# Gated attention and two MLPs on one core: U narrowed in the first attention chunk, half of the shifts on ScalarE, pair 2 through PSUM

## The chip, the cores and the metric

The kernel runs on one core of one Trainium2 chip. The metric is the device time of one execution in microseconds (us); lower is better. The time given for a kernel is the median of its runs.

## The reference

The input is four batches of 768 positions. Three parts follow each other:

- A gated linear attention over 8 heads of 48. With `f = sigmoid(f_logit)`, the state is `state = f[t] * state + outer(k[t], v[t])`, and the output is `y[t] = q[t] @ state`. The heads side by side give `x` (768 x 384).
- A low-rank mix over positions and an MLP: `u = x + (x^T @ U @ V)^T` with rank 32, then `x = u + relu(u @ w_ch1) @ w_ch2` with a hidden width of 1536.
- A gated block: `h = gelu(x @ w_in)` is cut in two halves, one half is normalised and mixed over positions by `w_sg`, the halves are multiplied, `w_out` follows, and `x` is added.

The weights U, V, w_ch1, w_ch2, w_in and w_out arrive as float64. The kernel takes them apart itself, as 64-bit words, since the chip computes in 32 bits.

## The kernel before, in words

**Order.** The program runs the attention of batch 0 alone, in six chunks of 128 positions (loop over `c`, lines 569 to 594). Then for each batch b come two half-batches (`hf`) of the first MLP, each in twelve steps `f`; between the matmuls of these steps the attention of batch b+1 is filled in by `plan` (lines 628 to 652). The third part follows at the end. From line 554 on the order is written out by hand: each engine executes its instructions in the order in which the program lists them, and an instruction that waits holds up all that stand behind it on its engine.

**Narrowing.** A float64 tile lies in SBUF as pairs of 32-bit words, `low` and `high`. Four small operations make a float32 tile of it:

- `spread` (line 253): ScalarE rescales the high word into `z`.
- `shift` (line 246): the low word is shifted right by 29 bits. VectorE does it (line 251), or ScalarE does the same from the word's top byte (line 249; before the change for U and for the first half of V, `"u"` and `"v0"`).
- `merge` (line 257): two VectorE instructions (lines 260 and 261) join `z` and `low`, then the sign.

`use_first` is spread and shift with `z` in SBUF, `use_middle` the merge. `bank_first` and `bank_middle` (lines 301 and 306) do the same with `z` in two PSUM banks. `use_last` (line 278) splits the result into a rounded high part (ScalarE, line 290) and a rest (GpSimd, line 292); for U it is `load_u` (line 310), where ScalarE repeats U four times (line 313) and VectorE makes the rest of one copy (line 314). "Pair i" below is the two tiles of MLP step i, w_ch1's and w_ch2's; there are twelve, 0 to 11. They go through only once, ahead of and during batch 0's first half, and stay in SBUF.

**Where each is narrowed.** U in chunk 1, V's halves in chunks 2 and 3, pair 0 in chunk 4, pair 1 in chunks 4 and 5, pair 2 behind the last chunk (lines 601 and 602), pairs 3 to 11 by `narrow_ahead` (line 618) during steps 0 to 8 of the first half: in step f, pair f+3 is merged, pair f+2 gets its `use_last`, and pair f+4 its `bank_first`.

**Between attention and MLP.** `low_rank_sum(0, c)` (line 470) adds `U^T x` of a chunk on TensorE, in a bank kept open. The last one gives `hs` (lines 480 and 481). `add_ahead` and `hl_from` (lines 494 to 508) build `u` of the first half of batch 0 in the three `"at"` banks, split it into `uh` (ScalarE) and `ul` (VectorE), and copy it to `xT` (line 507). The copy is read again only at the end of the half.

**A step of the MLP** (`mlp`, line 512): nine matmuls into `ps_h` (line 81); ScalarE takes the relu `ah` (line 542), VectorE the rest `al` (line 543); then TensorE runs the nine matmuls of the previous step's second layer (line 523, into `ps_ch`), and then the step's fill follows. In steps 2 to 4 of batch 0's first half the fill has also one low-rank product for the second half (`low_rank_add`, lines 490 and 492).

**Banks.** PSUM has eight: two `"h"`, three `"ch"`, three `"at"`. A tile gets the bank that has been free longest; its first writer waits until the last reader of the tile before is done. The attention of batch 0 uses `"ch"` for its outputs and transposes and `"at"` for scans and scores.

Of the kernel before, what the change touches and what calls it, by code (L numbers as in the profile page):

```python
# [8 lines left out]
F32 = mybir.dt.float32  # L9
# [4 lines left out]
ACTF = mybir.ActivationFunctionType  # L14
ALU = mybir.AluOpType
# [12 lines left out]
KD = DM // 128  # L28
KF1 = FF1 // 128
KH = HF // 128  # L30
HT = S // 2
# [6 lines left out]
UNIT = 384  # L38
ALL = slice(None)
# [13 lines left out]
def kernel(  # L53
# [16 lines left out]
    vec, act, pool, pe = nc.vector, nc.scalar, nc.gpsimd, nc.tensor  # L70
# [62 lines left out]
    def fast(st):  # L133
# [5 lines left out]
        xT = [keepx.tile([128, KD, S], F32, name=f"xT{b}") for b in range(B)]  # L139

        def bank(kind, shape):
            n = {"h": 2, "ch": 3, "at": 3}[kind]
            return ps.tile(shape, F32, tag=kind, bufs=n, name="ps_" + kind)
# [27 lines left out]
        zs = at_cm.enter_context(sp("zs", 2, "right"))  # L171
# [16 lines left out]
        us = cst.tile([128, NCH, 128], F32R, name="us")  # L188
# [38 lines left out]
        raws = {}  # L227
# [16 lines left out]
                    raws[i].append((words[:, :, 0], words[:, :, 1], tops[:, :, 3]))  # L244

        def shift(i):
            for low, _, top in raws[i]:
                if i in ("u", "v0"):
                    act.activation(low, top, ACTF.Copy, scale=1.0 / 32, bias=-15.5 / 32)
                else:  # L250
                    vec.tensor_scalar(low, low, 29, None, op0=ALU.logical_shift_right)  # L251
# [2 lines left out]
            for z, (_, high, _) in zip(zs, raws[i]):  # L254
                act.activation(z, high.bitcast(F32), ACTF.Copy, scale=2.0 ** -112)

        def merge(i, dst, zs):
            for d, z, (low, high, _) in zip(dst, zs, raws[i]):
                di, zi = d.bitcast(I32), z.bitcast(I32)
                vec.scalar_tensor_tensor(zi, zi, 3, low, op0=ALU.logical_shift_left, op1=ALU.bitwise_or)  # L260
                vec.scalar_tensor_tensor(di, high, -2 ** 31, zi, op0=ALU.bitwise_and, op1=ALU.bitwise_or)  # L261

        ready = {}

        def z_tiles(i):
            z = zs.tile([128, 2, UNIT], F32, tag="z", name="z")
            n = NCH * R if i == "u" else UNIT
            return [z[:, x, :n] for x in range(len(raws[i]))]

        def use_first(i):  # L270
            ready[i] = z_tiles(i)
            spread(i, ready[i])
            shift(i)

        def use_middle(i):
            merge(i, ready[i], ready[i])

        def use_last(i):
            del raws[i]
            z = ready.pop(i)  # L280
            if i == "u":
                load_u(z[0])
            elif i in homes:
                load_v(int(i[1]) * UNIT, z[0])
            else:
                hl = [p.tile([128, 2, UNIT], F32R, tag=f"w{i}", name=n + str(i)) for p, n in ((w1p, "w1"), (wp, "w2"))]
                w1s[i] = [hl[0][:, x].rearrange("p (a b) -> p a b", a=KD) for x in range(2)]
                w2s[i] = [hl[1][:, x] for x in range(2)]
                for t, s in zip(hl, z):
                    act.activation(t[:, 0], s, ACTF.Copy)  # L290
                for t, s in zip(hl, z):
                    pool.tensor_tensor(t[:, 1], s, t[:, 0].bitcast(F32), op=ALU.subtract)  # L292
# [5 lines left out]

        banked = {}

        def bank_first(i):
            banked[i] = [bank("at", [128, UNIT]) for _ in range(2)]
            spread(i, banked[i])
            shift(i)

        def bank_middle(i):
            ready[i] = z_tiles(i)
            merge(i, ready[i], banked.pop(i))

        def load_u(z):  # L310
            z3 = z.rearrange("p (c r) -> p c r", c=NCH)
            u4 = us.rearrange("p c (i r) -> p c i r", i=4)
            act.activation(u4, z3[:, :, None, :].to_broadcast([128, NCH, 4, R]), ACTF.Copy)
            vec.tensor_tensor(u4[:, :, 2, :], z3, u4[:, :, 2, :].bitcast(F32), op=ALU.subtract)

        def load_v(i, z):
            c = slice(i, i + UNIT)
# [71 lines left out]
        def a_out(b, c):  # L389
            e = tiles[b, c]  # L390
            vv = e["v"]
            y = bank(kind(b), [128, DM])
            half = [slice(i, i + C // 2) for i in range(0, C, C // 2)]
            for h in range(H):
                for t in half:
                    pe.matmul(y[t, h * D:(h + 1) * D], lhsT=e["am"][h % 2][:, h // 2, t],  # L396
                              rhs=vv[:, h * D:(h + 1) * D], start=(h == 0), stop=(c == 0 and h == H - 1))
            if c:
                for p in range(NP):
                    for t in half:  # L400
                        pe.matmul(y[t, p * 2 * D:(p + 1) * 2 * D], lhsT=e["q"][:, p, t], rhs=T[:, p, :],  # L401
                                  start=False, stop=(p == NP - 1))
            x = aw.tile([128, DM], F32, tag="x", name="x", bufs=3)
            act.activation(x, y, ACTF.Copy)
            if b:
                xh[b, c] = aw.tile([128, DM], F32R, tag="xh", name="xh", bufs=3)
                xl[b, c] = aw.tile([128, DM], F32R, tag="xl", name="xl", bufs=3)
                split(xh[b, c], xl[b, c], x)
            else:
                xh[b, c] = x  # L410
            if c < NCH - 1:
                kv = bank(kind(b), [PR, NP, D] if b else [PR, NP, 2 * D])
                if not b:
                    for rows in (slice(0, 64), slice(64, PR)):
                        pe.matmul(kv[rows], lhsT=ident[:PR, rows], rhs=T, start=True, stop=False)
                for p in range(NP):
                    for j in range(2):
                        rows = slice(64 * j, 64 * j + D)
                        pe.matmul(kv[rows, p, :] if b else kv[rows, p, j * D:(j + 1) * D], lhsT=e["kt"][:, p, rows],  # L419
                                  rhs=vv[:, (2 * p + j) * D:(2 * p + j + 1) * D], start=bool(b),  # L420
                                  stop=bool(b) or p == NP - 1)
                e["kv"] = kv
            e["x"] = x
# [70 lines left out]
        def add_ahead(d):  # L494
            t = bank("at", [128, HT])
            pe.matmul(t, lhsT=ident, rhs=xT[0][:, d, 0:HT], start=True, stop=False)
            return t

        def hl_from(us):
            hi = work.tile([128, KD, HT], F32R, tag="uh", name="uh")  # L500
            lo = work.tile([128, KD, HT], F32R, tag="ul", name="ul")
            for d, t in enumerate(us):
                pe.matmul(t, lhsT=hs[0][:, d * 128:(d + 1) * 128], rhs=vs[:, 0:HT], start=False, stop=True)
            for d, t in enumerate(us):
                split(hi[:, d], lo[:, d], t, vec)
            for d, t in enumerate(us):
                act.activation(xT[0][:, d, 0:HT], t, ACTF.Copy)
            hl[0, 0] = (hi, lo)

        pend = [lambda: None]  # L510
# [54 lines left out]
        a_scores(0, 0)  # L565
        warm(2)
        a_decay(0, 2)
        inside = {1: "u", 2: "v0", 3: "v1", 4: 0}
        for c in range(NCH):
            if c + 2 < NCH:  # L570
                a_grow(0, c + 2)
            if c + 1 < NCH:
                a_scores(0, c + 1)
            if c:
                a_xt(0, c - 1)
            if c > 1:
                low_rank_sum(0, c - 2)
            if c in inside:
                use_first(inside[c])
                use_middle(inside[c])  # L580
            elif c == NCH - 1:
                low_rank_sum(0, c - 1)
                use_middle(1)
            a_out(0, c)
            if c + 3 < NCH:
                a_decay(0, c + 3)
            if c + 1 < NCH:
                a_state(0, c)
            if c == NCH - 1:
                use_last(0)  # L590
            elif c == NCH - 2:
                use_first(1)
            elif c in inside:
                use_last(inside[c])
        sums_up = [add_ahead(d) for d in range(1)]
        low_rank_sum(0, NCH - 1)
        use_last(1)
        sums_up += [add_ahead(d) for d in range(1, KD)]
        hl_from(sums_up)
        a_xt(0, NCH - 1)  # L600
        use_first(2)
        use_middle(2)
        load(1, 0)
        load(1, 1)
        get(*range(3, KF1))
        bank_first(3)

        def rest(b, c):
            a_xt(b, c)
# [6 lines left out]
                load(nb, nc3)  # L616

        def narrow_ahead(f):
            if 2 <= f < 2 + KD:
                low_rank_add(0, 1, f - 2, "at")  # L620
            if f + 3 < KF1:
                bank_middle(f + 3)
            if f + 2 < KF1:
                use_last(f + 2)
            if f + 4 < KF1:
                bank_first(f + 4)
# [370 lines left out]
```

## Time and profile before

| | us |
|---|---|
| median of 3 runs | 697.84 |
| lowest, highest | 697.01, 699.84 |
| the profiled execution | 696.48 |
| its span, first to last instruction | 694.7 |

| engine | busy us | share of the span |
|---|---|---|
| TensorE (PE) | 678.2 | 98% |
| VectorE (DVE) | 424.2 | 61% |
| ScalarE (ACT) | 266.6 | 38% |
| GpSimd (POOL) | 244.9 | 35% |

Times in rows are counted from the start of the span. In the rows L470 is line 470 of the kernel, `out<-in` the tiles written and read, `x9` the number of instructions put together in one row. A bracket at the end of a row tells how long the engine was idle before it and which instruction ended that. PEld is TensorE's weight load, SPq the queue of DMA issues.

### The profile page before, as it was taken

The page shows a single profiled execution, that of the slowest core. Times are in us where ns is not written, and L with a number is a line of the kernel's source. Part 1 is how long each engine was busy: PE and PEld are TensorE (multiplying, and loading weights), DVE is VectorE, ACT ScalarE, POOL GpSimd, SP SyncE. Part 2 cuts the span into 40 slices and gives each one's busy share as a digit, 9 for nine tenths or more (in the row PEclk, how much of TensorE's full clock was granted, in tenths as well). Part 3 has the DMA queues.
Part 4 walks back from the last instruction along what each step waited for, and adds up shares of the span by engine and source line. Part 5 has one row for each costly group of instructions (what it writes and reads, how often), then busy time and mean ns, then how long its engine had stood idle before and what let it go on. Part 6 is the DMA issues. An engine that isn't in the chain of part 4 may idle for free.

```text
span 694.7 us, 12756 instructions
## 1 busy us (share of the span) xinstructions
PE 678.2 (98%) x5155; PEld 641.5 (92%) x5155; DVE 424.2 (61%) x745; ACT 266.6 (38%) x551; POOL 244.9 (35%) x302
## 2 busy tenths in 40 slices
PE   8898999999999999999999999999999999999996
PEld 5667989999999999999999999899899999989996
DVE  7989996645546535546538841585675386358532
ACT  4685623331333232333234533563434255243410
POOL 5535742221321120421122542675344353435030
PEclk9999999999999999999999999999999999999999
DMA  9990013130122110130005421000010001001002
GB/s 327 395 385 8 1 59 115 58 115 0 59 75 97 59 58 1 58 108 9 1 4 162 121 69 58 23 1 1 0 69 1 1 0 69 1 1 68 1 1 73
DMA packets 21810, 47.10 MB, mean 68 GB/s; under 512 B 2544, under 2 KB 10352, under 8 KB 21744
## 3 DMA queue, kind: packets, MB, share of 16 engines
q1 hardware_dynamic: 21744, 46.21, 19.4%
q8 instruction: 42, 0.69, 0.4%
q14 instruction: 24, 0.20, 0.1%
HBM read 41.49 MB, written 4.72 MB: 67 GB/s over the span
## 4 chain that ended last, share of the span: by engine, by line
PE 86%; DMA 7%; DVE 5%; issue 0%; POOL 0%; ACT 0%; SPq 0%; DVEq 0%; ACTq 0%
PE ps_h L81 29%; PE ps_ch L523 19%; PE ps_ch L81 13%; PE ps_at L81 13%; DMA raw<-in_w_dram 4%; PE ps_at L369 3%; PE ps_at L396 3%; DVE z L261 2%; PE ps_at L401 1%; DVE ps_at L260 1%; PE ps_at L383 1%; DVE raw L251 1%; DMA xT<-in_fqk_dram 1%; PE ps_at L470 1%; PE ps_at L446 1%; PE ps_at L419 1%
## 5 line engine op out<-in xcount | busy, mean ns | idle before, releaser
L543 DVE SCALAR_TENSOR_TENSOR al<-ps_h,ah 128x384 fp32r<-128x384 f32 x96 | 53.3, 556 | 117.0 <-ACT ah L542 116.5
L81 PE MATMUL ps_h<-uh,w 128*128 128x384 f32 x576 | 120.5, 343 | 0.7 <-POOL w L292 0.7
L523 PE MATMUL ps_ch<-ah,w 128*128 128x384 f32 x576 | 115.5, 334 | 1.0 <-ACT ah L542 1.0
L523 PEld LDWEIGHTS ps_ch<-ah,w 128*128 128x128 f32 x576 | 101.1, 188 | 1.5 <-ACT ah L542 1.5
L81 PEld LDWEIGHTS ps_h<-uh,w 128*128 128x128 f32 x576 | 98.9, 188 | 2.8 <-POOL w L292 1.0
L542 ACT ACTIVATE ah<-ps_h 128x384 fp32r<-128x384 f32 x96 | 47.1, 490 | 121.7 <-PE ps_h L81 121.7
L523 PE MATMUL ps_ch<-al,w 128*128 128x384 f32 x288 | 65.8, 336 | 1.0 <-DVE al L543 1.0
L81 PE MATMUL ps_h<-ul,w 128*128 128x384 f32 x288 | 65.4, 334 | 0.0
L147 POOL TENSOR_TENSOR ul<-xT,uh 128x384 fp32r<-128x384 f32 x45 | 46.8, 1067 | 47.7 <-ACT uh L146 46.8
L147 POOL TENSOR_TENSOR gtl<-t,gth 128x384 fp32r<-128x384 f32 x32 | 32.7, 1024 | 73.6 <-ACT gth L146 73.6
L523 PEld LDWEIGHTS ps_ch<-al,w 128*128 128x128 f32 x288 | 51.2, 188 | 1.4 <-DVE al L543 1.3
L81 PEld LDWEIGHTS ps_h<-ul,w 128*128 128x128 f32 x288 | 51.5, 188 | 0.1
L342 POOL TENSOR_TENSOR fall<-g,fqk 112x4 f32<-112x4 f32 x18 | 3.7, 207 | 134.7 <-DVE g L338 134.7
L146 ACT ACTIVATE gth<-t 128x384 fp32r<-128x384 f32 x32 | 16.8, 525 | 78.0 <-DVE t L775 78.0
L375 DVE TENSOR_TENSOR am<-ps_at,mask 128x512 f32<-128x512 f32 x42 | 27.3, 685 | 19.5 <-PE ps_at L369 19.4
L147 POOL TENSOR_TENSOR vnl<-t,vnh 128x512 fp32r<-128x512 f32 x24 | 31.0, 1292 | 17.8 <-ACT vnh L146 17.8
L81 PE MATMUL ps_ch<-w,vnh 128*128 128x384 f32 x144 | 36.6, 335 | 0.0
L81 PE MATMUL ps_at<-w,vnh 128*128 128x384 f32 x144 | 36.6, 334 | 0.0
L147 POOL TENSOR_TENSOR xl<-x,xh 128x384 fp32r<-128x384 f32 x18 | 18.2, 1010 | 51.8 <-ACT xh L146 50.5
L292 POOL TENSOR_TENSOR w<-z,w 128x384 fp32r<-128x384 f32 x24 | 24.4, 1036 | 18.9 <-ACT w L290 15.0
L345 POOL TENSOR_TENSOR fqk<-fqk,g 112x512 f32<-112x512 f32 x21 | 27.0, 1285 | 6.7 <-DVE g L338 6.7
L369 PEld LDWEIGHTS ps_at<-fqk 48*128 48x128 f32 x336 | 21.7, 187 | 7.5 <-issue 4.4
(225 smaller groups left out, 1502.3 us busy)
## 6 DMA issues: line engine op xcount, KB each, us to landing
fqk<-in_fqk_dram SPq DMA_DIRECT2D x38, 384.0 KB, 3.8
raw<-in_w_dram SPq DMA_DIRECT2D x24, 384.0 KB, 7.8
out_dram<-xT SPq DMA_DIRECT2D x24, 192.0 KB, 1.9
v<-in_v_dram SPq DMA_DIRECT2D x21, 192.0 KB, 4.1
raw<-in_w_in_dram SPq DMA_DIRECT2D x8, 384.0 KB, 3.2
xT<-in_fqk_dram SPq DMA_DIRECT2D x6, 384.0 KB, 6.5
z<-in_w_sg_dram SPq DMA_DIRECT2D x12, 192.0 KB, 2.4
fqk<-in_fqk_dram SPq DMA_DIRECT2D x6, 256.0 KB, 4.7
```

The source lines that it names most:

```text
L81: pe.matmul(ps, lhsT=l, rhs=r, start=(i == 0), stop=(i == n - 1))
L146: act.activation(hi, src, ACTF.Copy)
L147: eng.tensor_tensor(lo, src, hi.bitcast(F32), op=ALU.subtract)
L261: vec.scalar_tensor_tensor(di, high, -2 ** 31, zi, op0=ALU.bitwise_and, op1=ALU.bitwise_or)
L292: pool.tensor_tensor(t[:, 1], s, t[:, 0].bitcast(F32), op=ALU.subtract)
L345: pool.tensor_tensor(k, k, g.rearrange("p h t -> p (h t)"), op=ALU.mult)
L369: pe.matmul(sc[j][:, p, :], lhsT=e["k"][rows, p, :], rhs=e["q"][rows, p, :], start=True, stop=True)
L375: vec.tensor_tensor(am, sc[j], m3, op=ALU.mult)
L396: pe.matmul(y[t, h * D:(h + 1) * D], lhsT=e["am"][h % 2][:, h // 2, t], rhs=vv[:, h * D:(h + 1) * D], start=(h == 0), stop=(c == 0 and h = ...
L523: pe.matmul(ch[d], lhsT=w, rhs=a[i // 2], start=(f == 0 and i == 0), stop=(last and i == 2))
L542: act.activation(ah, hp, ACTF.Relu)
L543: vec.scalar_tensor_tensor(al, hp, 0.0, ah.bitcast(F32), op0=ALU.max, op1=ALU.subtract)
```

## The change

1. `load_u`: the subtraction for U goes from VectorE to GpSimd.
2. U is narrowed one chunk sooner: spread and shift ahead of chunk 0's work, merge and `load_u` in chunk 0 instead of chunk 1.
3. `shift`: ScalarE takes also V's second half, and of each pair from 3 on the first tile (w_ch1's). VectorE keeps the second tile, and both tiles of pairs 0, 1 and 2.
4. Pair 2: spread (into one `"h"` and one `"ch"` bank) and shift in the last attention chunk; the two merges around `hl_from`; its `use_last` first in the fill of step 0.
5. The three copies to `xT` go from `hl_from` to the fill of step 0, behind the first relu; `bank_first(3)` follows them there, since the three `"at"` banks are taken until then.

```diff
         def shift(i):
-            for low, _, top in raws[i]:
-                if i in ("u", "v0"):
+            for x, (low, _, top) in enumerate(raws[i]):
+                if i in ("u", "v0", "v1") or i > 2 and x == 0:
                     act.activation(low, top, ACTF.Copy, scale=1.0 / 32, bias=-15.5 / 32)
                 else:
                     vec.tensor_scalar(low, low, 29, None, op0=ALU.logical_shift_right)
...
-        def bank_first(i):
-            banked[i] = [bank("at", [128, UNIT]) for _ in range(2)]
+        def bank_first(i, kinds=("at", "at")):
+            banked[i] = [bank(k, [128, UNIT]) for k in kinds]
             spread(i, banked[i])
             shift(i)
...
-            vec.tensor_tensor(u4[:, :, 2, :], z3, u4[:, :, 2, :].bitcast(F32), op=ALU.subtract)
+            pool.tensor_tensor(u4[:, :, 2, :], z3, u4[:, :, 2, :].bitcast(F32), op=ALU.subtract)
...
                 split(hi[:, d], lo[:, d], t, vec)
-            for d, t in enumerate(us):
-                act.activation(xT[0][:, d, 0:HT], t, ACTF.Copy)
             hl[0, 0] = (hi, lo)
...
-        inside = {1: "u", 2: "v0", 3: "v1", 4: 0}
+        inside = {0: "u", 2: "v0", 3: "v1", 4: 0}
         for c in range(NCH):
+            if c == 0:
+                use_first("u")
             if c + 2 < NCH:
                 a_grow(0, c + 2)
...
             if c in inside:
-                use_first(inside[c])
+                if c:
+                    use_first(inside[c])
                 use_middle(inside[c])
             elif c == NCH - 1:
                 low_rank_sum(0, c - 1)
                 use_middle(1)
+                bank_first(2, ("h", "ch"))
             a_out(0, c)
...
         low_rank_sum(0, NCH - 1)
         use_last(1)
-        sums_up += [add_ahead(d) for d in range(1, KD)]
-        hl_from(sums_up)
+        bank_middle(2, slice(0, 1))
+        ups += [add_ahead(d) for d in range(1, KD)]
+        hl_from(ups)
+        bank_middle(2, slice(1, 2))
         a_xt(0, NCH - 1)
-        use_first(2)
-        use_middle(2)
         load(1, 0)
         load(1, 1)
         get(*range(3, KF1))
-        bank_first(3)
...
         def narrow_ahead(f):
+            if f == 0:
+                use_last(2)
+                for d, t in enumerate(ups):
+                    act.activation(xT[0][:, d, 0:HT], t, ACTF.Copy)
+                bank_first(3)
             if 2 <= f < 2 + KD:
                 low_rank_add(0, 1, f - 2, "at")
             if f + 3 < KF1:
                 bank_middle(f + 3)
-            if f + 2 < KF1:
+            if 0 < f < KF1 - 2:
                 use_last(f + 2)
```

## Rows read from the trace of the kernel before

**Rows 1.** Busy by stretch: stretch, its us, each engine's busy us, PEclk, DMA share, GB/s

```profile
22.90:25.30 2.40, 0.03 (x2) 0.02 (x1) 2.40 (x2) 2.11 (x5) 2.11 (x3) 1.00 1.04 397
25.30:46.50 21.20, 21.20 (x322) 15.54 (x322) 18.07 (x29) 14.00 (x37) 8.71 (x9) 1.00 1.03 395
92.00:424.00 332.00, 331.14 (x2930) 318.81 (x2929) 189.04 (x323) 107.50 (x220) 84.56 (x106) 1.00 0.21 65
```

**Rows 2.** Timeline of TensorE, 22 to 27 us: start us, us, instruction

```profile
22.42 0.49 PE L446 MATMUL ps_ch<-ident,x 128*128 128x128 f32 x3
25.28 0.91 PE L470 MATMUL ps_h<-x,us 128*128 128x384 f32 x2 [2.37 <-DVE us L314]
```

**Rows 3.** Timeline of VectorE and GpSimd, 22 to 26 us

```profile
22.87 2.36 DVE L314 TENSOR_TENSOR us<-z,us 128x192 fp32r<-128x192 f32 x1 [0.28 <-ACT us L313]
23.74 1.27 POOL L378 TENSOR_TENSOR am<-am,mask 128x512 f32<-128x512 f32 x1
```

**Rows 4.** Timeline of ScalarE, 47 to 56 us

```profile
47.06 1.41 ACT L507 ACTIVATE xT<-ps_at 128x384 f32<-128x384 f32 x3
...
50.51 0.49 ACT L542 ACTIVATE ah<-ps_h 128x384 fp32r<-128x384 f32 x1
...
54.97 0.48 ACT L542 ACTIVATE ah<-ps_h 128x384 fp32r<-128x384 f32 x1
```

**Rows 5.** Timeline of TensorE, 47 to 76 us

```profile
47.70 0.74 PE L81 MATMUL ps_h<-ul,w 128*128 128x384 f32 x3
...
51.05 1.33 PE L523 MATMUL ps_ch<-ah,w 128*128 128x384 f32 x6 [1.02 <-ACT ah L542]
...
58.81 0.44 PE L490 MATMUL ps_at<-vs,hs 128*128 128x384 f32 x1 [1.41 <-DVE z L261]
...
62.47 0.44 PE L490 MATMUL ps_at<-vs,hs 128*128 128x384 f32 x1
...
72.67 1.20 PE L81 MATMUL ps_h<-uh,w 128*128 128x384 f32 x6
...
75.79 1.20 PE L81 MATMUL ps_h<-uh,w 128*128 128x384 f32 x6
```

**Rows 6.** Timeline, 62 to 91 us: VectorE, and TensorE's wait

```profile
62.33 0.63 DVE L251 TENSOR_SCALAR raw<-raw 128x384 int32<-128x384 int32 x2
...
80.10 1.54 DVE L251 TENSOR_SCALAR raw<-raw 128x384 int32<-128x384 int32 x2
...
85.47 1.62 DVE L338 TENSOR_TENSOR_SCAN g<-fqk,gone 112x511 f32<-112x511 f32 x1 [0.71 <-ACT fqk L331]
...
90.52 1.16 PE L369 MATMUL ps_at<-fqk 48*128 48x128 f32 x16 [1.02 <-POOL gmin L346]
```

**Rows 7.** Groups by line and shape, 11 to 92 us: busy, mean ns | idle before, releasers

```profile
L292 POOL TENSOR_TENSOR w<-z,w 128x384 fp32r<-128x384 f32 x24 | 24.4, 1036 | 18.9 <-ACT w L290 15.0 <-DMA raw<-in_w_dram 3.8
L251 DVE TENSOR_SCALAR raw<-raw 128x384 int32<-128x384 int32 x25 | 12.2, 530 | 0.0
L261 DVE SCALAR_TENSOR_TENSOR z<-raw,ps_at 128x384 int32<-128x384 int32 x18 | 10.0, 555 | 1.2
L255 ACT ACTIVATE ps_at<-raw 128x384 f32<-128x384 f32 x18 | 9.2, 517 | 9.9 <-DVE z L261 7.5 <-DVE xT L492 2.4
```

**Rows 8.** DMA issues of U: the timeline's row, and KB and us to landing

```profile
7.21 0.33 SPq L241 DMA_DIRECT2D raw<-in_w_u_dram  x1
...
raw<-in_w_u_dram SPq DMA_DIRECT2D x1, 192.0 KB, 5.4
```

**Rows 9.** Timeline of ScalarE and VectorE in the attention, single instructions

```profile
13.29 0.60 ACT L377 ACTIVATE am<-ps_at 128x512 f32<-128x512 f32 x1 [1.27 <-PE ps_at L369]
24.42 0.59 ACT L249 ACTIVATE raw<-raw 128x384 int32<-128x384 uint8 x1
42.82 0.49 ACT L404 ACTIVATE x<-ps_ch 128x384 f32<-128x384 f32 x1 [1.15 <-PE ps_ch L401]
44.84 0.55 DVE L481 TENSOR_TENSOR hs<-ps_h,hs 32x384 fp32r<-32x384 f32 x1 [1.31 <-ACT hs L480]
```

More of the change, by code (lines that the diff above doesn't have):

```diff
@@ L255, in spread, with merge @@
                 act.activation(z, high.bitcast(F32), ACTF.Copy, scale=2.0 ** -112)
-        def merge(i, dst, zs):
-            for d, z, (low, high, _) in zip(dst, zs, raws[i]):
+        def merge(i, dst, zs, only=ALL):
+            for d, z, (low, high, _) in list(zip(dst, zs, raws[i]))[only]:
                 di, zi = d.bitcast(I32), z.bitcast(I32)
@@ L299, in fast, with bank_middle @@
         banked = {}
-        def bank_first(i):
-            banked[i] = [bank("at", [128, UNIT]) for _ in range(2)]
+        def bank_first(i, kinds=("at", "at")):
+            banked[i] = [bank(k, [128, UNIT]) for k in kinds]
             spread(i, banked[i])
             shift(i)
-        def bank_middle(i):
-            ready[i] = z_tiles(i)
-            merge(i, ready[i], banked.pop(i))
+        def bank_middle(i, only=ALL):
+            if i not in ready:
+                ready[i] = z_tiles(i)
+            merge(i, ready[i], banked[i], only)
         def load_u(z):
@@ L594, in fast @@
                 use_last(inside[c])
-        sums_up = [add_ahead(d) for d in range(1)]
+        ups = [add_ahead(0)]
         low_rank_sum(0, NCH - 1)
         use_last(1)
-        sums_up += [add_ahead(d) for d in range(1, KD)]
-        hl_from(sums_up)
+        bank_middle(2, slice(0, 1))
+        ups += [add_ahead(d) for d in range(1, KD)]
+        hl_from(ups)
+        bank_middle(2, slice(1, 2))
         a_xt(0, NCH - 1)
-        use_first(2)
-        use_middle(2)
         load(1, 0)
```

## The prediction, made before the changed kernel was run

> **What bounds the kernel now.** First the table of busy time by stretch [rows 1]. From 92 us to 424 us TensorE is busy in 331.14 of 332.00 us, and the change touches nothing there, so the question is the first 92 us. The stretch from 22.90 to 25.30 us stands out: TensorE does almost nothing in it. Right behind it, from 25.30 to 46.50 us, it is busy without a gap (21.20 of 21.20 us) while VectorE (18.07) and ScalarE (14.00) have room. So in the attention TensorE waits once and then sets the pace to the end.
>
> The timeline names that wait: the first low-rank sum, line 470, starts at 25.28 us after 2.37 us of idling for `us`, VectorE's subtraction on line 314 [rows 2]. That subtraction has 192 columns and takes 2.36 us, from 22.87 to 25.23 us; it ends just after GpSimd's mask product, which runs from 23.74 to 25.01 us [rows 3]. It does not compute for 2.36 us, it is held up by GpSimd's work.
>
> Next the entry of the MLP. Step 0's first layer is done at 48.44 us (47.70 + 0.74), but its relu `ah` starts only at 50.51 us: ScalarE first does three copies to `xT` (1.41 us), pair 2 and pair 3. The relu of step 1 starts at 54.97 us [rows 4, 5]. TensorE waits 1.02 us for the first relu, and at 58.81 us 1.41 us for a merge on VectorE, whose bank the low-rank product needs. Steps 2 and 3 with such a product take 3.66 us (62.47 - 58.81), plain steps 3.12 us (75.79 - 72.67), which is TensorE's own pace [rows 5].
>
> Last, at the end of the narrowing, a pair of shifts that takes 0.63 us undisturbed takes 1.54 us; a scan idles 0.71 us for a sigmoid, and TensorE waits 1.02 us ahead of the first scores of batch 1 [rows 6].
>
> The chain of waits is no help before 48 us: it runs through DMAs that had landed long before their readers started.
>
> **The change part by part.**
>
> *U sooner, and its subtraction on GpSimd.* With `us` ready, the sum on line 470 follows the transposes that end at 22.91 us (22.42 + 0.49), 2.37 us sooner [rows 2]. On GpSimd the subtraction costs some 0.52 us, half of the 1036 ns of 384 columns on line 292 [rows 7]; it stands ahead of a mask product that is read a whole chunk later. VectorE loses the 2.36 us and keeps U's two merges, a chunk earlier. Since TensorE was gapless from there on, the whole of it should arrive at the end of the attention: **-2.4 us**. Between the ends, 0 (another wait takes the place) and -2.4, I take the upper one because VectorE, which feeds TensorE, loses as much.
>
> The Trainium skill (GPSIMD Engine Reference, section 4.1 Engine selection) says otherwise for such an operation: elementwise work belongs on VectorE, GpSimd being about twice as slow with two inputs. By it this edit would lose some 0.26 us and the sum would be about -1.0 us. The row decides against it: 2.36 us on VectorE here.
>
> New waits by it: ScalarE's spread for U now waits for U's DMA with all of chunk 0 queued behind it. It is issued at 7.21 us and lands 5.4 us later, at 12.6 us [rows 8]. ScalarE idles 1.27 us before 13.29 us [rows 9], and the two short instructions fit almost exactly. Each us of later landing would push the attention by up to one, of which VectorE's 2.4 us of new room takes some. No DMA changes its place in SP's queue.
>
> *V's second half shifted by ScalarE.* 0.59 us more there [rows 9], a shift less on VectorE; TensorE is the bound in that chunk [rows 1], so 0. Were ScalarE late, 0.6 us at most.
>
> *Pair 2 in the last chunk.* Two spreads of 0.52 us come ahead of the copy at 42.82 us, before which ScalarE idles 1.15 us; two shifts on VectorE come ahead of the subtraction at 44.84 us, before which it idles 1.31 us [rows 9]. Cost 0; with the cover gone some 0.1 to 0.5 us. The first half of the merge has the gap behind that subtraction, the second the one ahead of `al` of step 0. Both banks are free: the last chunk holds two of three `"ch"` and one of two `"h"`.
>
> *The entry.* The relu of step 0 now starts when its matmuls are done, at 48.44 - 2.37 = 46.07 us, and the first wait of 1.02 us is gone. But its queue behind that relu has grown: `ah`, two copies of pair 2, three copies to `xT`, two spreads of pair 3 and two of pair 4, ten instructions at 0.46 us from start to start (the three copies: (1.41 - 0.49) / 2), and two shifts at 0.5 us. The second spread of pair 4 waits for a bank that the merge of pair 3's first tile frees, two instructions of 0.555 us [rows 7] behind ScalarE's own shift, less the 0.46 us of the first spread: 0.65 us idle. Together 4.6 + 1.0 + 0.65 = 6.25 us, so the relu of step 1 starts at 52.3 us, not 54.97: -2.65 us in all, and beyond the attention's share only **-0.3 us**. Then VectorE does `al` and four merges: 0.49 + 0.55 + 4 x 0.555 us, with small overlaps 3.25 us; the low-rank product starts at 55.6 us, not 58.81: another **-0.5 us**. Ends for both: +0.5 (a wait of ScalarE's usual 1.1 us, below) and -1.5 us (no such wait).
>
> *The steps.* VectorE's sum falls by one shift of 0.3 us, to 3.35 us with a product. But ScalarE's shift now closes a loop: second spread 0.52, shift 0.59, relu 0.48, `al` 0.55, product 0.55, the first tile's merge 1.11, and again; 3.8 us, less four overlaps of 0.1 and three handovers of 0.05 added, 3.55 us. In plain steps 3.1 us, beside TensorE's 3.12. So **-0.2 us** for two steps; ends -0.6 (VectorE's sum) and +0.6 (no overlap). Step 6 has three more copies on ScalarE for the next half and no room for them in this loop: **+0.2 us**, between 0 and 1.4 (three at 0.46).
>
> *The end of the narrowing.* One shift instead of two can be held up, so the last merges, the sigmoid and the scan come sooner relative to TensorE, which recovers part of its 1.02 us [rows 6]: **-0.5 us**, between 0 and -1.0.
>
> Beyond 92 us: 0, with 0.5 us either way for where GpSimd and VectorE happen to meet.
>
> **Sum:** -2.4 - 0.3 - 0.5 - 0.2 + 0.2 - 0.5 = **-3.7 us**, so 692.8 us for the profiled execution (696.48 us). The median of the runs is 1.36 us above that one, so the forecast for the median is 697.84 - 3.7 = **694.1 us**.
>
> **The rivals.**
>
> *The stall only moves.* With `us` early, something else holds the second chunk. For: VectorE is nearly full there, 2.40 of 2.40 us [rows 1]. Against: 2.36 of these are the stall itself. Half of the -2.4 lost gives 695.3, all of it 696.5.
>
> *The entry gives nothing.* ScalarE's queue in step 0 is longer than I count (6.25 us with a guess for the wait), and what the steps win goes to it. The attention's share alone remains: about 695.4.
>
> *ScalarE closes the loop on every step* (slower). Its spreads idled 9.9 us for VectorE [rows 7], over nine steps 1.1 us each, harmless so far. If that wait stays while a shift is added, a step is 0.48 + 4 x 0.517 + 0.59 us less five overlaps of 0.1, so 2.6, plus 1.1: 3.7 us against 3.12 in six plain steps, +3.5 us. With -2.4 - 0.8, +0.2 and no recovery at the end that is +0.5 us: 698.3. It decides where the second spread of a pair waits for a merge that starts behind ScalarE's own shift. For: that shift stands last in ScalarE's step. Against: the merge of pair f+3 needs a shift of the step before. The Trainium skill (ScalarE: Activation LUTs, section Rules for kernel authors) sides with this rival: simple arithmetic belongs on VectorE, not on ScalarE.
>
> *The change doesn't do what it says.* Pairs 0 to 2 keep both shifts on VectorE, so "one tile of each pair" holds for nine pairs of twelve; that is counted. 2%.
>
> **How the numbers follow.** Two runs of this kernel can be told apart at about 0.5%, 3.49 us here, so faster means below 694.35. The forecast lies 0.25 us under that. It has 0.55 (0.44 of it below 694.35), the moved stall 0.17, the idle entry 0.18, the ScalarE loop 0.08, the last 0.02. Faster 0.47 (0.03 from the others), same 0.48, slower 0.05 (the loop together with a late U). The range goes down to -4.8 us (entry -1.5, end -1.0 and part of the steps) and up to -0.6 us, where the moved stall and the idle entry meet in part: 693.0 to 697.2.
>
> **What would show it.** Right: line 470 starts near 22.9 us with no wait; TensorE gapless to the MLP; the first `ah` near 46.1 and the second near 52.3 us; the low-rank product at 55.6; steps with a product at 3.55 us; a wait under 0.6 us ahead of batch 1's scores, which start near 86.8. Wrong: a new gap of TensorE between 12 and 44 us; the second `ah` at 52.6 or later; plain steps over 3.2 us.

## The result, and the profile after

The changed kernel takes 691.60 us (median of 4 runs, 691.03 to 692.40); the kernel before took 698.38 us beside it (4 runs, 697.01 to 699.84). The ratio is 0.9903, interval 0.9879 to 0.9928: faster by 6.8 us. Forecast were 694.1 us and a range of 693.0 to 697.2 us, so the sign is right, the size too small, and the range missed it.

The two profiled executions lie closer together than the medians: 696.48 us before, 692.03 us after (spans 694.7 and 690.2 us), 4.5 us apart. The remaining 2.3 us is no part of a comparison of these two traces. Where it comes from is the main question of the experiments.

First the attention. Busy time by stretch, after:

```profile
22.90:25.30 2.40, 2.40 (x52) 1.78 (x52) 2.37 (x4) 1.56 (x5) 2.00 (x3) 1.00 1.04 399
25.30:46.50 21.20, 21.20 (x286) 15.86 (x282) 19.40 (x34) 16.91 (x44) 9.87 (x10) 1.00 1.03 395
```

and the timelines of TensorE at the first low-rank sum (line 471 now), of GpSimd at U's subtraction, of ScalarE at U's spread:

```profile
22.28 0.49 PE L447 MATMUL ps_ch<-ident,x 128*128 128x128 f32 x3
22.61 0.81 PE L471 MATMUL ps_h<-x,us 128*128 128x384 f32 x2
...
19.23 0.60 POOL L315 TENSOR_TENSOR us<-z,us 128x192 fp32r<-128x192 f32 x1
...
12.75 0.37 ACT L255 ACTIVATE z<-raw 128x192 f32<-128x192 f32 x1 [0.88 <-DMA raw<-in_w_u_dram]
```

The stretch in which TensorE did nothing [rows 1] is filled, and the sum follows the transposes without a wait. The subtraction takes 0.60 us on GpSimd, against 2.36 us on VectorE [rows 3]. ScalarE waits 0.88 us for U's DMA with chunk 0 behind it, as the prediction feared, but TensorE is busy for all of 12 to 22 us, so it costs nothing.

Next the entry and the steps. Timelines of ScalarE, VectorE and GpSimd from 41 to 53 us:

```profile
41.54 0.49 ACT L481 ACTIVATE hs<-ps_h 128x384 fp32r<-128x384 f32 x1 [0.18 <-PE ps_h L471]
...
45.80 0.49 ACT L541 ACTIVATE ah<-ps_h 128x384 fp32r<-128x384 f32 x1 [1.01 <-PE ps_h L81]
...
47.02 1.24 ACT L624 ACTIVATE xT<-ps_at 128x384 f32<-128x384 f32 x3
...
50.86 0.52 ACT L255 ACTIVATE ps_at<-raw 128x384 f32<-128x384 f32 x1 [0.89 <-DVE z L261]
51.31 0.54 ACT L249 ACTIVATE raw<-raw 128x384 int32<-128x384 uint8 x1
51.74 0.48 ACT L541 ACTIVATE ah<-ps_h 128x384 fp32r<-128x384 f32 x1
...
46.80 1.22 DVE L251 TENSOR_SCALAR raw<-raw 128x384 int32<-128x384 int32 x1
49.60 0.57 DVE L260 SCALAR_TENSOR_TENSOR ps_at<-ps_at,raw 128x384 int32<-128x384 int32 x1 [1.58 <-ACT raw L249]
...
46.78 2.11 POOL L292 TENSOR_TENSOR w<-z,w 128x384 fp32r<-128x384 f32 x2 [1.85 <-ACT w L290]
```

Of VectorE and ScalarE the groups by line, 11 to 92 us, that changed most:

```profile
L251 DVE TENSOR_SCALAR raw<-raw 128x384 int32<-128x384 int32 x15 | 7.9, 541 | 0.0
L255 ACT ACTIVATE ps_at<-raw 128x384 f32<-128x384 f32 x18 | 9.2, 519 | 5.6 <-DVE z L261 4.8 <-DVE xT L493 0.8
```

VectorE has ten shifts less [rows 7], and ScalarE's spreads idle 5.6 us instead of 9.9. TensorE, 46 to 87 us:

```profile
46.67 0.68 PE L81 MATMUL ps_h<-ul,w 128*128 128x384 f32 x3
...
52.27 1.31 PE L522 MATMUL ps_ch<-ah,w 128*128 128x384 f32 x6 [1.80 <-ACT ah L541]
...
55.06 0.44 PE L491 MATMUL ps_at<-vs,hs 128*128 128x384 f32 x1 [0.95 <-DVE z L261]
...
58.65 0.44 PE L491 MATMUL ps_at<-vs,hs 128*128 128x384 f32 x1
...
79.25 1.20 PE L81 MATMUL ps_h<-uh,w 128*128 128x384 f32 x6
...
82.37 1.20 PE L81 MATMUL ps_h<-uh,w 128*128 128x384 f32 x6
...
85.99 1.16 PE L370 MATMUL ps_at<-fqk 48*128 48x128 f32 x16 [0.34 <-issue]
```

The lead over before, event by event, begins with `hs`, for which the row of before is this:

```profile
44.32 0.49 ACT L480 ACTIVATE hs<-ps_h 128x384 fp32r<-128x384 f32 x1 [0.18 <-PE ps_h L470]
```

`hs` comes at 41.54 instead of 44.32 us (2.78 us), the second relu at 51.74 instead of 54.97 (3.23) [rows 4], the first low-rank product at 55.06 instead of 58.81 (3.75) [rows 5], the first scores of batch 1 at 85.99 instead of 90.52 (4.53) [rows 6]. From there to the end the lead stays what it is: the last instruction of VectorE starts at 684.40 instead of 688.95 us (4.55). From the end of that instruction to the end of the span the twelve profiles need 4.4 to 5.6 us, so two spans can differ by 1 us by that end alone; where it matters below, profiles are compared at that instruction instead. The wait for the first relu is gone; the one for the second is now the longest, 1.80 us, because ScalarE carries more between the two relus. Plain steps keep TensorE's pace (82.37 - 79.25 = 3.12 us).

### The profile page after: what moved, and what is told of

It reads as the page before. It is cut to its first block, busy times and chain, and to the rows that moved or that the text cites. A ratio compares the mean times of both kernels' runs of the same rounds, so it can differ in the third digit from the quotient of the medians.

```text
span 690.2 us, 12745 instructions
## 1 busy us (share of the span) xinstructions
PE 677.4 (98%) x5155; PEld 641.4 (93%) x5155; DVE 418.5 (61%) x734; ACT 270.9 (39%) x561; POOL 244.8 (35%) x303
## 4 chain that ended last, share of the span: by engine, by line
PE 93%; DVE 3%; ACT 2%; issue 1%; POOL 1%; DMA 0%; DVEq 0%; POOLq 0%; ACTq 0%
PE ps_h L81 30%; PE ps_ch L522 20%; PE ps_ch L81 14%; PE ps_at L81 14%; PE ps_at L370 4%; PE ps_at L397 3%; PE ps_at L402 1%; PE ps_at L384 1%; PE ps_at L471 1%; PE ps_ch L397 1%; PE ps_at L447 1%; PE ps_at L420 1%; ACT raw L249 1%; DVE z L261 1%; PE ps_h L471 1%
```

## The experiments

Three theories stood for the 2.3 us between medians and profiles:

- **Clock.** In most runs of the kernel before, TensorE falls to half clock behind its 2.4 us of idling for `us`; the profiled execution was one in which it didn't. The change takes that away too.
- **Held instructions.** The runs of before differ in how long VectorE's instructions are held up by GpSimd's.
- **Other parts.** The entry or the shifts bring more in most runs than in the profiled one.

The expectations of the first set of runs were written before the clock was suspected; it became a theory with that set's first profile. Times are medians; the kernel before had 698.03, 697.68 and 697.79 us beside the three sets of runs.

### The kernel before once more (first set)

No edit.

> The kernel before, unchanged, beside itself. It is to show what its runs differ by: its profiled execution took 696.48 us, its median 1.9 us more. Theory A (the parts gave what the profiles show, -4.5 us, and the rest of the difference between the medians is the spread of the kernel before): ratio 1.000 within 0.002, single runs 696.5 to 700, and a profile that differs from the earlier one inside the first 92 us by up to 2 us, in how long blocked VectorE instructions take. Theory B (the profiles miss something after 92 us that the change also moved): the first 92 us agree within 0.5 us and what differs lies later.

Measured: 698.41 us (12 runs, 696.74 to 699.87), ratio 1.0001 [0.9990, 1.0013]. The profiled execution was a typical one this time, 698.97 us with a span of 697.2 us. Its timeline shows the same wait, and its table by stretch (TensorE's busy time and granted clock, the last but two of the numbers) what follows it:

```profile
25.28 1.01 PE L470 MATMUL ps_h<-x,us 128*128 128x384 f32 x1 [2.38 <-DVE us L314]
```

```profile
22.90:25.30 2.40, 0.02 (x2) 0.85 1.04 397
25.30:26.30 1.00, 1.00 (x2) 0.50 1.05 393
26.30:30.30 4.00, 4.00 (x51) 0.50 1.03 394
30.30:31.30 1.00, 1.00 (x8) 0.50 1.04 393
31.30:32.30 1.00, 1.00 (x27) 0.95 1.04 397
```

The granted clock falls before the wait is over (0.85 in the first row) and is 0.50 for some 6 us behind it (1.2 GHz, the lower of the two levels), where the first profile of before had 1.00 in all of it [rows 1]. VectorE's subtraction lasts as long as ever (2.37 us from 22.86 us). The first relu,

```profile
53.35 0.49 ACT L542 ACTIVATE ah<-ps_h 128x384 fp32r<-128x384 f32 x1
```

comes 2.84 us later than the 50.51 us of the first profile [rows 4], about half of the 6 us, and the last instruction of VectorE 2.89 us later (691.84 against 688.95). So between these two executions the difference arises ahead of the MLP, by the clock and not by held instructions. The other runs have a mean granted clock each, and it goes with their time: of the 64 runs of this kernel in the three sets, the eleven with 0.999 or more took 695.31 to 696.74 us, the fifty with 0.997 or less 696.93 to 699.87 us.

The Trainium skill (TensorE: Matmul & The Clock Gate, Part 1, "What's actually happening") puts it so: "the default state is throttled, and activity releases the throttle." The rows above agree, with the two levels it names; that the same 2.4 us gap brings the fall in one execution and not in another is what the two profiles of before add.

### Only U sooner (first set)

The kernel before with parts 1 and 2 of the change alone:

```diff
-            vec.tensor_tensor(u4[:, :, 2, :], z3, u4[:, :, 2, :].bitcast(F32), op=ALU.subtract)
+            pool.tensor_tensor(u4[:, :, 2, :], z3, u4[:, :, 2, :].bitcast(F32), op=ALU.subtract)
...
-        inside = {1: "u", 2: "v0", 3: "v1", 4: 0}
+        inside = {0: "u", 2: "v0", 3: "v1", 4: 0}
         for c in range(NCH):
+            if c == 0:
+                use_first("u")
```

> The kernel before with parts 1 and 2 of the change alone (U in chunk 0, its subtraction on GpSimd). By the forecast -2.4 us, all of it at the low-rank sum of chunk 0, which then starts near 22.8 us, and no more later: ratio 0.9965. If the stall only moved: ratio over 0.998. If the U parts carry most of the measured 6.8 us: ratio 0.993 or less.

Measured: 693.19 us (5 runs, 692.74 to 693.82), ratio 0.9933 [0.9918, 0.9948]: 4.8 us, twice the length of the wait, and the runs spread over 1.1 us instead of 3. In its profile the clock is 1.00 from 12 to 92 us. The first low-rank product,

```profile
56.04 0.44 PE L490 MATMUL ps_at<-vs,hs 128*128 128x384 f32 x1 [1.41 <-DVE z L261]
```

comes 2.77 us sooner than in the profile of before [rows 5]. So 2.8 us of the 4.8 are the stall, and some 2.1 us aren't in a comparison with an execution that kept its clock.

### Without the shifts, and without the new entry (first set)

The changed kernel with the shifts of pairs 3 to 11 on VectorE again (V's second half stays on ScalarE):

```diff
-                if i in ("u", "v0", "v1") or i > 2 and x == 0:
+                if i in ("u", "v0", "v1"):
```

> The changed kernel with both shifts of pairs 3 to 11 back on VectorE (V's second half stays on ScalarE). If ScalarE's queue in step 0 is the bound there, as forecast, two shifts less bring the second relu 1.0 us sooner, from 51.7 to 50.7 us, and the steps are then 3.66 us instead of 3.59 where they have a product; at the end of the narrowing two shifts can be held up again, 0.5 to 0.9 us: the same time as the changed kernel within 1 us. If the shifts on ScalarE are what freed VectorE from GpSimd (the rival): 2 us or more slower than the changed kernel.

Measured: 691.93 us (691.41 to 692.40), ratio 0.9914 [0.9899, 0.9929]. And with parts 4 and 5 taken back, so that U and the shifts are left:

```diff
-                bank_first(2, ("h", "ch"))
...
-        bank_middle(2, slice(0, 1))
-        ups += [add_ahead(d) for d in range(1, KD)]
-        hl_from(ups)
-        bank_middle(2, slice(1, 2))
+        sums_up += [add_ahead(d) for d in range(1, KD)]
+        hl_from(sums_up)
         a_xt(0, NCH - 1)
+        use_first(2)
+        use_middle(2)
...
+        bank_first(3)
...
-            if f == 0:
-                use_last(2)
-                for d, t in enumerate(ups):
-                    act.activation(xT[0][:, d, 0:HT], t, ACTF.Copy)
-                bank_first(3)
```

> The changed kernel with parts 4 and 5 undone: pair 2 and the copies to xT as before, U and the shifts as changed. Forecast: the second relu is 0.3 to 1 us later than in the changed kernel (the relu of step 0 near 48.5 us, the one of step 1 near 52.5 us), and the kernel slower than the changed one by 0.8 us; if the blocked shift of pair 3 (1.44 us for two in the kernel before) stays, by 1.5 us. If the entry is worth nothing, the same time.

Measured: 691.29 us (690.76 to 691.73), ratio 0.9905 [0.9890, 0.9920], so not the 0.8 us above the changed kernel that were forecast: at least level with it. TensorE's waits at the entry, first without the shifts, then with the old entry:

```profile
51.15 1.32 PE L522 MATMUL ps_ch<-ah,w 128*128 128x384 f32 x6 [0.78 <-ACT ah L541]
54.46 0.44 PE L491 MATMUL ps_at<-vs,hs 128*128 128x384 f32 x1 [1.40 <-DVE z L261]
```

```profile
48.63 1.32 PE L523 MATMUL ps_ch<-ah,w 128*128 128x384 f32 x6 [1.46 <-ACT ah L542]
54.81 0.44 PE L490 MATMUL ps_at<-vs,hs 128*128 128x384 f32 x1 [0.93 <-DVE z L261]
```

On top of U alone the shifts bring 1.9 us (693.19 - 691.29) and the entry 1.3 us (693.19 - 691.93). Both together bring 1.6 us (the ratios 0.9933 and 0.9903 are 2.1 us apart, the two spans 691.8 and 690.2 us 1.6). They don't add: the first product comes at 54.46 us with the entry alone, 54.81 with the shifts alone and 55.06 with both. What the shifts bring on their own lies there (56.04 to 54.81) and in the 1.0 us ahead of batch 1's scores, which the kernel without shifts keeps and the one with the old entry doesn't.

### U's subtraction on VectorE, one chunk sooner (second set)

```diff
-            pool.tensor_tensor(u4[:, :, 2, :], z3, u4[:, :, 2, :].bitcast(F32), op=ALU.subtract)
+            vec.tensor_tensor(u4[:, :, 2, :], z3, u4[:, :, 2, :].bitcast(F32), op=ALU.subtract)
```

> The changed kernel with U's subtraction back on VectorE, still in chunk 0. It then queues behind VectorE's scan for chunk 3 and runs against GpSimd's products. If the engine is what mattered: the subtraction is held up by 1 to 2.5 us again and delays the scores of chunk 3, a wait of TensorE of 1 to 2 us near 21 us, and the kernel is 1 to 4 us slower than the changed one (the larger if the clock falls too). If the earlier place alone does it: the same time as the changed kernel.

Measured: 695.29 us (10 runs, 693.42 to 698.17), ratio 0.9966 [0.9947, 0.9986], 3.7 us of the gain gone (against 691.60 us; the two ratios are 4.4 us apart, `hs` in the two profiles 3.98 us, 45.52 against 41.54). Timelines of VectorE and TensorE, and the stretch behind:

```profile
17.91 2.73 DVE L315 TENSOR_TENSOR us<-z,us 128x192 fp32r<-128x192 f32 x1
...
22.61 1.71 PE L370 MATMUL ps_at<-xT 48*128 48x128 f32 x16 [1.87 <-issue]
...
25.00:30.00 5.00, 5.00 (x72) 0.66 1.04 395
```

The prediction's rival "the stall only moves" is what happens here. VectorE is held for 2.73 us, until 20.64 us, just behind GpSimd's three instructions, which run from 17.79 to 20.44 us; the scan, the products and the mask behind it come late, TensorE idles 1.87 us ahead of the next scores, and the clock falls behind that as well. The runs lie between 693.42 us, with a mean granted clock of 1.0, and 698.17 us with 0.99. So the earlier place alone doesn't remove the stall; what the engine does without it is the next question.

### U on GpSimd, but in chunk 1 as before (second set)

```diff
-        inside = {0: "u", 2: "v0", 3: "v1", 4: 0}
+        inside = {1: "u", 2: "v0", 3: "v1", 4: 0}
         for c in range(NCH):
-            if c == 0:
-                use_first("u")
```

> The changed kernel with U back in chunk 1, its subtraction on GpSimd. There it stands behind the key product of chunk 4 (to 23.6 us) and takes 0.5 us: the low-rank sum starts near 24.3 us, TensorE waits 1.4 us instead of 2.4 or none. 1.4 us slower than the changed kernel if the clock stays, up to 4 us if it falls behind a wait of that length as well. If the place doesn't matter: the same time as the changed kernel.

Measured: 693.29 us (5 runs, 692.69 to 693.50), ratio 0.9940 [0.9919, 0.9962].

```profile
24.27 0.91 PE L471 MATMUL ps_h<-x,us 128*128 128x384 f32 x2 [1.47 <-POOL us L315]
...
25.00:30.00 5.00, 5.00 (x93) 1.00 1.03 394
```

The subtraction stands behind a decay product on GpSimd and TensorE waits 1.47 us. The clock stays in this profile. `hs` comes 1.77 us later than with the whole change (43.31 against 41.54 us), the last instruction of VectorE 1.69 us (686.09 against 684.40), and the medians are as far apart (693.29 and 691.60 us): this shorter gap cost about its own length. So the engine alone leaves some 1.5 us of the wait, and it takes the engine and the earlier place together to remove it.

### The wait filled with products that nobody reads (second set)

The kernel before, with idle products in TensorE's queue ahead of the first low-rank sum. They are extra work; their results go nowhere.

```diff
+            if c == 2:
+                warm(3)
             if c > 1:
                 low_rank_sum(0, c - 2)
```

> The kernel before with three products of the identity with itself (some 2.2 us of TensorE work that nobody reads) ahead of the low-rank sum of chunk 0, where TensorE waits 2.4 us for U. The wait itself stays; only its idleness goes. Theory C (the idle wait costs twice: its 2.4 us, and in most runs a stretch behind it in which TensorE is granted half its clock, 0.50 from 25 to 31 us in the second profile of the kernel before, 2.5 us longer in all): the granted clock stays 1.00 from 22 to 46 us, the median falls to 696.6 us, ratio 0.998, and the runs lie within 1 us instead of 3. Rival (the clock has nothing to do with the spread of the runs): the same median and spread as the kernel before.

Measured: 696.12 us (12 runs, 695.34 to 696.49), ratio 0.9983 [0.9971, 0.9995].

```profile
22.42 2.10 PE L551 MATMUL ps_h<-ident 128*128 128x384 f32 x6
24.97 0.91 PE L470 MATMUL ps_h<-x,us 128*128 128x384 f32 x2 [0.44 <-DVE us L314]
...
26.30:30.30 4.00, 4.00 (x82) 1.00 1.04 397
```

This is the direct test of the clock. The low-rank sum still has to wait for `us`, starting 0.31 us sooner (by no work of the products: chunk 1's scores are 0.33 us sooner already, at 11.75 instead of 12.08 us), yet the median falls by 1.6 us and the spread from 4.3 us (24 runs of before beside it, 695.31 to 699.59) to 1.15 us. The lowest run is the same, 695.34 against 695.31; only the long ones are gone: 18 of the 24 runs of before lie above the highest of these twelve. The profiled execution is the lowest of the twelve, so its full clock proves little by itself; the spread of the twelve says more. Extra work makes this kernel faster.

### ScalarE's shifts only from pair 5 on (second set)

```diff
-                if i in ("u", "v0", "v1") or i > 2 and x == 0:
+                if i in ("u", "v0", "v1") or i > 4 and x == 0:
```

> The changed kernel with the shift of the first tile on ScalarE only from pair 5 on; pairs 3 and 4, whose shifts stand in step 0 between the first and the second relu, are shifted by VectorE. If ScalarE's queue in step 0 (5.9 us from relu to relu in the changed kernel) is the bound there: the second relu comes 1.0 us sooner, near 50.7 us, the wait of TensorE ahead of it shrinks from 1.8 to 0.8 us, and the kernel is 0.5 to 1.0 us faster than the changed one, near 690.8 us. If VectorE, which then has two shifts against GpSimd, is the next bound: the same time.

Measured: 691.41 us (6 runs, 690.50 to 691.46), ratio 0.9912 [0.9892, 0.9932]: no difference that can be told.

```profile
46.77 2.30 DVE L251 TENSOR_SCALAR raw<-raw 128x384 int32<-128x384 int32 x2
...
51.21 1.32 PE L522 MATMUL ps_ch<-ah,w 128*128 128x384 f32 x6 [0.79 <-ACT ah L541]
54.52 0.44 PE L491 MATMUL ps_at<-vs,hs 128*128 128x384 f32 x1 [1.40 <-DVE z L261]
```

The second relu comes 1.05 us sooner, at 50.69 us, but the product then waits 1.40 us for VectorE, whose two shifts are held until GpSimd's rests (46.75 to 48.85 us) are done. Of what ScalarE gives up, VectorE takes half: the product comes 0.54 us sooner (54.52 against 55.06), and the last instruction of VectorE 0.60 us (683.80 against 684.40). That is too little for the medians to show beyond their noise.

### The changed kernel once more, and the copies on VectorE (third set)

The changed kernel without an edit:

> The changed kernel, unchanged, for a comparison on one chip with the next run and for its own spread. If the spread of the kernel before comes from the clock behind the idle wait, which the changed kernel hasn't: runs within 1.5 us, median 691.0 to 692.0 us, ratio 0.9905 to 0.9925, and a granted clock of 1.00 from 12 to 92 us.

Measured: 691.94 us (6 runs, 691.40 to 693.27), ratio 0.9915 [0.9896, 0.9934]. That is 5.9 us below the kernel before (697.79 us), where the first comparison gave 6.8, and still below the range forecast; the runs spread over 1.9 us, not the 1.5 expected. The profiled execution was the longest of them, span 691.4 us. TensorE's wait, its busy time and granted clock by stretch, coarse and then fine, and the first scores of batch 1:

```profile
52.31 1.33 PE L522 MATMUL ps_ch<-ah,w 128*128 128x384 f32 x6 [1.79 <-ACT ah L541]
...
46.00:58.90 12.90, 10.38 (x47) 0.80 0.51 197
58.90:69.00 10.10, 10.10 (x55) 0.92 0.00 0
...
53.00:53.50 0.50, 0.50 (x5) 1.00 0.19 71
53.50:54.00 0.50, 0.50 (x4) 0.79 0.15 50
...
87.92 1.16 PE L370 MATMUL ps_at<-fqk 48*128 48x128 f32 x16 [0.34 <-issue]
```

The expectation of a full clock from 12 to 92 us fails: the changed kernel has the same weakness at a smaller price. In this execution the clock falls between 53.5 and 54.0 us, over 1 us behind the end of its wait of 1.8 us for the second relu and ahead of the next wait. In its first profile the same wait left the clock at 1.00, and batch 1's scores came 1.93 us sooner (85.99 against 87.92 us); the spans are only 1.2 us apart. Then the three copies to `xT` behind the first relu by VectorE:

```diff
                 for d, t in enumerate(ups):
-                    act.activation(xT[0][:, d, 0:HT], t, ACTF.Copy)
+                    vec.tensor_copy(xT[0][:, d, 0:HT], t)
```

> The changed kernel with the three copies to xT, behind the first relu, done by VectorE instead of ScalarE. In the changed kernel ScalarE is busy or waiting for 5.9 us between the relus of steps 0 and 1, 1.2 us of it these copies, while VectorE idles 1.6 us there. If ScalarE's queue is the bound of that step: the second relu near 50.9 us instead of 51.74, TensorE's wait ahead of it 1.0 us instead of 1.8, and 0.8 us faster than the changed kernel. If VectorE's merges for pair 3 are the bound: no faster, and the second relu stays within 0.3 us.

Measured: 691.29 us (6 runs, 690.39 to 691.47), ratio 0.9905 [0.9886, 0.9924].

```profile
51.44 1.31 PE L522 MATMUL ps_ch<-ah,w 128*128 128x384 f32 x6 [1.11 <-ACT ah L541]
54.22 0.44 PE L491 MATMUL ps_at<-vs,hs 128*128 128x384 f32 x1 [0.95 <-DVE z L261]
```

VectorE idled 1.58 us there anyway, ScalarE's queue is three copies shorter, and the wait for the second relu falls to 1.11 us. The product comes 0.84 us sooner (54.22 against 55.06), the last instruction of VectorE 0.81 us (683.59 against 684.40), as expected. All six runs have a mean granted clock of 0.999. It is the best version by its median, 0.65 us under the changed kernel on the same chip and level with the one with the old entry; its highest run, 691.47, is about the changed kernel's lowest, 691.40, though the two ratios' intervals overlap.

## Why the prediction was wrong in size

**The step that failed** is the first term with what was hung on it: "-2.4 us", with 0 and -2.4 as its ends, and then "the median of the runs is 1.36 us above that one", added back unchanged. The term counted TensorE's idling alone and took the clock behind it from one execution, where it was 1.00 [rows 1]. That execution was a fortunate one: it lay below all three runs shown. The 1.36 us between it and the median was no constant of measuring (after the change the median lies 0.43 us below the profiled execution) but, for the most part, the half clock behind the very wait that the change removes. In medians U alone is worth 4.8 us: 2.8 of stall and about 2 of clock (1.6 by the idle products, 2.1 by U alone). The runs of before reached from 697.01 to 699.84 us; nothing was made of that spread, nor of the profiled execution's place below it, and these were the only signs of it among the data.

**The stall itself** measured 2.78 us at `hs`, not 2.4. TensorE's line 470 starts 2.86 us behind its transposes before [rows 2], line 471 0.33 us behind them after, a gain of 2.53 us: an idle time in brackets is counted from the modelled end of pipelined matmuls, which a next matmul needn't await (line 471 starts at 22.61 us, the row of its transposes ends at 22.77). 0.14 us more is no work of the change: chunk 1's scores start that much sooner already, at 11.94 instead of 12.08 us; in the three profiles that leave this part as before they start between 11.75 and 12.08. The last 0.11 us lies in the sum itself: from its start to that of the next matmuls it is 0.85 us before (25.28 to 26.13) and 0.74 us after (22.61 to 23.35).

**The Trainium skill's rule on the engine** (GPSIMD Engine Reference, section 4.1 Engine selection) would have given about -1.0 us by the prediction's estimate. The runs decide against it for this place: 0.60 us on GpSimd, 2.73 us on VectorE one chunk sooner. With GpSimd idle VectorE is the quicker one here too, as one of U's merges after the change shows, with as many columns and both inputs in SBUF:

```profile
15.91 0.35 DVE L260 SCALAR_TENSOR_TENSOR z<-z,raw 128x192 int32<-128x192 int32 x1
```

Another line of the same page of the Trainium skill (section 8 Key points) fits the place better: GpSimd contends with VectorE instructions that run in what it calls a 2-port perf mode or have two SBUF inputs. Lines 314 and 315 on VectorE have two, and both end 0.2 us behind GpSimd's work.

**The entry:** -0.3 and -0.5 us forecast; measured -0.45 (3.23 - 2.78) and -0.52 (3.75 - 3.23). From relu to relu it is 5.94 us, not 6.25, although ScalarE's wait for the merge was 0.89 us, not 0.65. Right in the sum, but what it is worth depends on the shifts: the two compete for ScalarE between the same two relus, and taking back either one alone costs nothing that can be told.

**Steps, step 6 and the end:** -0.2, +0.2 and -0.5 us forecast, together -0.5; measured -0.78 (4.53 - 3.75). A step with a product takes 3.59 us (58.65 - 55.06), forecast 3.55. Over the steps with a product the lead grows from 3.75 to 3.90 us; at step 6 it falls to 3.65, as forecast; a wait for GpSimd's rest that is 0.2 us shorter (0.46 instead of 0.68 us) brings it to 3.85, which was no term of the sum; and the wait ahead of batch 1's scores, down from 1.02 to 0.34 us, to 4.53.

So without the clock the sum was -3.7 against a measured -4.5 us; of the difference 0.4 us is the stall and 0.4 us the rest. **The slower rival**, ScalarE closing the loop on every step, did not happen: ScalarE idles 5.6 us for its spreads instead of 9.9 [rows 7], and plain steps stay at 3.12 us. **That the stall only moves** is true of VectorE and not of GpSimd.

What stays open: why the same wait brings the lower clock in one execution and not in the next; and whether each of the longer runs lost its time in this place, since only profiled executions show the clock by stretch (with the idle products, runs of 696.05 us have a mean of 0.995 as well, so the mean alone doesn't tell).

## What to carry to other kernels

Price an idle gap of TensorE with the clock behind it, and not from one execution: where runs of the same kernel spread over several us, look for a gap ahead of dense work, and ask whether the profiled execution lies at the low end. If the gap can't be closed, filling it with idle products may win back the clock. And when two edits put work on one engine between the same two deadlines, measure each without the other: here either one alone gave what both gave.

## What the runs showed that was not expected

A gap of 2.4 us of TensorE cost 4.8 us in the median, about twice its length; one of 1.5 us cost about its own length; behind one of 1.8 us, ahead of the second relu's product, the clock fell in one of the four profiles that have it (both of the changed kernel, U on VectorE, U in chunk 1), for 1.9 us more; behind one of 1.87 us it fell in the one profile that has it.

VectorE's larger operations from SBUF to SBUF were held by GpSimd whether they had one input or two. The shift on line 251, with one, takes 0.35 us undisturbed, but 1.22 us at 46.80 us and 2.30 us for two of them at 46.77 us, each ending about 0.2 us behind one of GpSimd's two rests (2.11 us together). Of those with two, a merge of V in the changed kernel takes 1.55 us instead of 0.55 (line 260, 128x384, at 30.31 us) and ends 0.42 us behind GpSimd's mask product (30.16 to 31.44 us), and the subtraction for U at 17.91 us was let through only behind three of GpSimd's instructions. Not held are the pairs' merges with `z` in PSUM, which keep their 0.56 us beside GpSimd's rests (52.71 to 54.70 us), and a reciprocal of four columns from SBUF to SBUF (line 344, 0.17 us at 22.28 us, beside a product of GpSimd from 22.25 us).
